# Attention heads paired by parity in 64x32 and 32x32 tiles of TensorE, part of the vector work on GpSimd in slots 24 to 103, and a Prelu step in the weight conversion

## The chip, the cores and the metric

One Trainium2 chip, of which the kernel uses one core. The metric is the time of one execution on the device in microseconds (us). In the text PE is TensorE, DVE is VectorE, ACT is ScalarE, POOL is GpSimd, SP is SyncE.

## The reference, cut to what matters

q, k and v have the shape (4, 8, 576, 64): 4 batches, 8 heads, 576 tokens, 64 columns. The attention result feeds two feed-forward layers whose weights are 64-bit floats in memory (512x2048 and 2048x512 each).

```python
q_lm = q.reshape(B, H, 32, 18, D).mean(axis=3)      # k_lm likewise
A = sm(q, k_lm); Bm = sm(q_lm, k_lm); C = sm(q_lm, k)   # sm: softmax of scaled scores
Z = Bm.transpose(0, 1, 3, 2) / (norm1(Bm) * norminf(Bm) + 1e-06)
for _ in range(6):
    Z = 2 * Z - Z @ Bm @ Z
x = (A @ Z @ C @ v)                 # tokens x 512
h = x @ w_in;  x = (h - tanh(h)) @ w_out            # first layer
h = x @ w_in2; x = (h * tanh(softplus(h))) @ w_out2 # second layer, the output
```

## The kernel before, in words

**Phase 1** is a pipeline of 128 slots, 32 for each batch: two halves of 288 tokens by 16 blocks of 128 hidden columns. The product A (Z C v) w_in is folded: for each batch and block of 512 hidden columns P = (Z C v) w_in is made per head, and h of a slot is P times the softmax A. Slot s makes h(s) with six matmuls of 128x288 (L489 to L491, in the type fp32r, each factor split into a high and a low part) and, with a lag of three slots, y(s-3) with twelve (L589, L590, L593) that accumulate over the 16 blocks. The vector work of a slot (`vec`) makes h - tanh h: ACT squares h (L539), takes its tanh (L540), an exponential (L542) and a square (L553); DVE makes a mask for small h (L545), h times its square (L549), h - tanh h (L550, which is also the last reader of the PSUM bank of h, of which there are two), and for the slot before the product L567 and the choice by the mask, L571. For slot s-2 the result g is split for the y matmuls: ACT writes the high part (L94), DVE the low one (L95, tile `gg`).

**Beside it** run parts of the attention for the next half or batch, as generators of which one piece is issued in a slot. `attn_pre` takes means of q and k (L220), makes the scores of the landmarks (L254), their softmax, C v in 32-wide column tiles (L339), and inverts Bm by Newton's steps: five iterations of L365, a 128x128 matmul of 192 columns for each of the two groups of four heads, and DVE's update L368. The four heads of a group stand in a block-diagonal matrix (L328). `attn_a` makes the scores of A (L404), and the softmax with a subtraction and a multiplication on GpSimd (L419, L431) and a split whose low part is GpSimd's too (L439, which calls L95). `p_gen` makes one P for a batch, a group and a block of 512 columns (L461, then ACT L469 and DVE L471); it runs in slots 1, 2, 5, 6 and 27, 28, 30, 31 of a batch.

**Weights** come as pairs of 32-bit words. A conversion makes fp32 of 128x512 of them: ACT takes the high words (L118) and the low ones (L122), DVE joins them in two scalar_tensor_tensor instructions (STT, L129 and L133). Of the 64 conversions 32 lie in the first 130 us, before and in slots 0 to 14, six in slots 105 to 122, and 26 in phase 2. Weights of w_out, and both weights of the second layer, are then split, the low part on GpSimd (L95).

**Phase 2** is the second layer in 96 slots of 384 tokens by 128 hidden columns, from 486 us on; its inputs are split by L778 with GpSimd.

**Order.** Up to slot 115 a list scheduler places the instructions on each engine, with higher priority for the split of gg, L567, L571 and ACT's exponential and square. From slot 116 (`SWITCH`) they stand as written.

Of the kernel before, what the change touches and what calls it, by code (L numbers as in the profile page):

```python
# [27 lines left out]
def kernel(  # L28
# [16 lines left out]
    M = 32  # L45
# [42 lines left out]
    G = nc.gpsimd  # L88

# [25 lines left out]

    def f32_a(raw, on_act):
        y = st_p.tile([128, 512], F32, tag="y", name="y")
        A.activation(out=y, in_=raw.bitcast(F32)[:, :, 1], func=ACTF.Copy, scale=2.0 ** -112)  # L118
# [7 lines left out]
        return y, lo  # L126

    def f32_b(y, lo, t):
# [4 lines left out]
        V.scalar_tensor_tensor(  # L133
            out=t.bitcast(U32), in0=y.bitcast(U32), scalar=0x80000000, in1=lo,
            op0=ALU.bitwise_and, op1=ALU.bitwise_or,
        )
        yield 0

    def split_job(src, pool, tag, dst, i):
        def done(y):  # L140
            w = pool.tile([128, 2, 512], F32R, tag=tag, name=tag)
            split(y, w[:, 0, :], w[:, 1, :], G)
            dst[i] = w
        return src, done, None

    def keep_job(src, g, j, a):
# [5 lines left out]
        def done(y):  # L152
            if a == 1:
                nc.sync.dma_start(out=w1s[g, j], in_=w1t[0, g, j])
                ready.append((g, j))
        return src, done, where

    def convert(jobs, act_share=1, more=None):
# [10 lines left out]
        for i in range(n + 2):  # L169
            if i < n:  # L170
                st[i], los[i] = f32_a(raws.pop(i), i % act_share == 0)
            if i - 1 in los:
                where = jobs[i - 1][2]
                yield from f32_b(st[i - 1], los.pop(i - 1), where() if where else st[i - 1])
# [7 lines left out]
    QB, KB, Z0 = [], [], []  # L182

    def setup_bd():
        for i in range(2):
            for lst, nm in ((QB, "qb"), (KB, "kb")):
                z = bd_p.tile([128, 4, 32], F32, tag=f"{nm}{i}", name=nm)
                G.memset(z, 0.0)
                lst.append(z)
        z = bd_p.tile([128, NG, 2, 64], F32, name="z")  # L190
        G.memset(z, 0.0)
        Z0.append(z)
# [21 lines left out]
    def attn_pre(b):  # L214
# [8 lines left out]
        def scaled(g, x):  # L223
            if x == 0:
                A.activation(out=ks[g][:, :, S:S + M], in_=red[:, g, 0], func=ACTF.Copy, scale=1.0 / R)
            for i in range(2):
                ps = slice(64 * i, 64 * i + 64)
                adone.add((b, g, "kq"[x]))
                A.activation(out=(KB, QB)[x][g][ps, i:4:2, :], in_=red[ps, g, x], func=ACTF.Copy, scale=1.0 / R)
# [17 lines left out]
        for hf in range(2):  # L247
            pp = []
            for g in range(NG):
                inp[b, g]["c"] = c[:, g]  # L250
                p = ps_m.tile([128, 512], F32, tag="m", name="m")
                qf = QB[g].rearrange("p a c -> p (a c)")
# [3 lines left out]
                pp.append(p)  # L256
# [50 lines left out]
        for g in range(NG):  # L307
# [18 lines left out]
        BD = sm_p.tile([128, 2 * NG, 4, M], F32, tag="BD", name="BD", bufs=1)  # L326
        bbv = bb.rearrange("p t (g o) m -> p (t g) o m", o=1)
        V.tensor_tensor(out=BD, in0=bbv.to_broadcast([128, 2 * NG, 4, M]),  # L328
                        in1=mask.rearrange("p (o a) m -> p o a m", o=1).to_broadcast([128, 2 * NG, 4, M]), op=ALU.mult)
# [3 lines left out]
        for g in range(NG):  # L333
            vv = inp[b, g]["v"]
            for j in range(5):
                n = 128 if j < 4 else 64
                for i in range(4):
                    c4 = slice(32 * i, 32 * i + 32)
                    mm(pv[c4, 64 * g:64 * g + 64], cts[g][0:n, j, c4], vv[0:n, j, 64 * i:64 * i + 64],  # L339
# [8 lines left out]
        yv = sm_p.tile([128, NG, 192], F32, tag="yv", name="yv", bufs=2)  # L348
        for g in range(NG):
            A.activation(out=yv[:, g, 128:192], in_=pv[:, 64 * g:64 * g + 64], func=ACTF.Copy,  # L350
# [3 lines left out]
        for g in range(NG):  # L354
            bt = BD[:, NG + g].rearrange("p a m -> p (a m)")
            mm(py[:, 128 * g:128 * g + 128], bt, bt, start=True, stop=True)
        yield 1
        nr = n4.rearrange("p t (g o) -> p t g o", o=1)[:, 3]
        V.tensor_tensor(out=yv[:, :, 0:128], in0=py[:, 0:256].rearrange("p (g n) -> p g n", g=NG),
                        in1=nr.to_broadcast([128, NG, 128]), op=ALU.mult)  # L360
        yield 1
        for it in range(5):
            pn = ps_m.tile([128, 512], F32, tag="m", name="m")
            for g in range(NG):
                mm(pn[:, 192 * g:192 * g + 192], yv[:, g, 0:128], yv[:, g], start=True, stop=True)  # L365
            yield 1
            y2 = sm_p.tile([128, NG, 192], F32, tag="yv", name="yv", bufs=2)
            V.scalar_tensor_tensor(out=y2, in0=yv, scalar=2.0, in1=pn[:, 0:192 * NG].rearrange("p (g n) -> p g n", g=NG),  # L368
# [4 lines left out]
        for g in range(NG):  # L373
            mm(pn[:, 64 * g:64 * g + 64], yv[:, g, 0:128], yv[:, g, 128:192], start=True, stop=True)
        yield 1
        v6 = sm_p.tile([128, NG, 64], F32, tag="v6", name="v6", bufs=1)
        V.scalar_tensor_tensor(out=v6, in0=yv[:, :, 128:192], scalar=2.0,
# [511 lines left out]
```

## Time and profile before

| | before |
|---|---|
| median of 3 runs | 889.87 us (885.38 to 890.6) |
| profiled execution, its own time | 888.02 us |
| span of the profiled execution | 886.1 us |
| PE busy | 834.0 us (94%) |
| DVE busy | 559.6 us (63%) |
| ACT busy | 512.8 us (58%) |
| POOL busy | 138.3 us (16%) |
| moved by DMA | 79.54 MB |

The busy time of an engine is summed over the whole span, so a share over the span says little about a kernel with stages: DVE's 63% is nearly all in the first 486 us. The table by stretches in the rows below is the view to begin with. In the rows, L12 is line 12 of the kernel before; x is a count of records; a matmul in fp32 leaves two records. PEclk is the granted clock of TensorE, 1.00 being the higher of its two levels, 2.4 GHz.

### The profile page before, as it was taken

How to read it: one execution, taken by the hardware profiler on the slowest of the kernel's cores; microseconds unless marked ns; L12 is line 12 of the kernel's file. 1: busy time of each engine (PE TensorE's matmuls, PEld its weight loads, DVE VectorE, ACT ScalarE, POOL GpSimd, SP SyncE). 2: the span in 40 equal slices, each digit the busy share in tenths (PEclk: the TensorE clock that was granted, in tenths of full speed). 3: DMA queues.
4: the chain of work that ended last, by engine and by line, in shares of the span. 5: the costliest groups of instructions: out<-in, count | busy, mean ns of one | idle time of the engine just before them, and what ended most of it. 6: DMA issues, size and time to landing. Idle time of an engine off the chain costs nothing.

```text
span 886.1 us, 13841 instructions
## 1 busy us (share of the span) xinstructions
PE 834.0 (94%) x5080; PEld 721.3 (81%) x5080; DVE 559.6 (63%) x1268; ACT 512.8 (58%) x1254; POOL 138.3 (16%) x131
## 2 busy tenths in 40 slices
PE   4678779999999999999889999999999999999998
PEld 2444669878997889878789978998998999899896
DVE  7898999999999999999995698611111111111111
ACT  6688977787877887789876667432311311311311
POOL 1431310220002100222310355411100100100000
PEclk8579999999999999999999999999999999999999
DMA  8788603151404300152201555101200200200000
GB/s 294 244 269 313 245 7 129 60 168 45 135 1 132 140 1 28 49 170 63 84 1 47 198 186 188 45 32 31 71 1 1 73 1 1 63 1 0 36 1 36
DMA packets 34916, 79.54 MB, mean 90 GB/s; under 512 B 5408, under 2 KB 14112, under 8 KB 34848
## 3 DMA queue, kind: packets, MB, share of 16 engines
q1 hardware_dynamic: 34848, 78.66, 26.7%
q8 instruction: 40, 0.66, 0.3%
q14 instruction: 28, 0.23, 0.1%
HBM read 65.01 MB, written 13.63 MB: 89 GB/s over the span
## 4 chain that ended last, share of the span: by engine, by line
PE 76%; DVE 14%; ACT 4%; DMA 2%; issue 2%; SPq 0%; POOL 0%; DVEq 0%; ACTq 0%
PE y L589 7%; PE y L617 6%; PE y L613 6%; PE y L612 6%; PE y L593 6%; PE y L590 6%; PE h L513 5%; PE h L515 5%; PE h L514 5%; PE h L489 3%; PE h L490 3%; PE h L491 3%; PE m L461 3%; DVE y L133 2%; PE m L515 2%; PE m L513 2%
## 5 line engine op out<-in xcount | busy, mean ns | idle before, releaser
L560 DVE TENSOR_TENSOR gg<-g,gg 128x384 fp32r<-128x384 f32 x96 | 58.3, 607 | 285.6 <-ACT g L559 285.3
L589 PE MATMUL y<-gg,w 128*128 128x288 f32 x512 | 151.4, 311 | 0.7 <-ACT gg L94 0.6
L590 PE MATMUL y<-gg,w 128*128 128x288 f32 x512 | 143.5, 296 | 0.0
L589 PEld LDWEIGHTS y<-gg,w 128*128 128x128 f32 x512 | 96.4, 188 | 30.4 <-issue 26.1
L593 PE MATMUL y<-gg,w 128*128 128x288 f32 x512 | 109.6, 299 | 5.7 <-DVE gg L95 5.6
L558 ACT ACTIVATE gg<-h 128x384 fp32r<-128x384 f32 x66 | 32.4, 491 | 125.8 <-PE h L515 125.8
L613 PE MATMUL y<-w,gg 128*128 128x512 f32 x256 | 101.2, 395 | 0.0
L612 PE MATMUL y<-w,gg 128*128 128x512 f32 x256 | 100.8, 394 | 0.0
L590 PEld LDWEIGHTS y<-gg,w 128*128 128x128 f32 x512 | 96.9, 189 | 0.8 <-issue 0.8
L593 PEld LDWEIGHTS y<-gg,w 128*128 128x128 f32 x512 | 81.5, 189 | 12.1 <-DVE gg L95 8.3
L617 PE MATMUL y<-w,gg 128*128 128x512 f32 x256 | 88.4, 396 | 0.0
L489 PE MATMUL h<-AT,P 128*128 128x288 f32 x256 | 78.5, 307 | 7.8 <-DVE th L550 7.4
L94 ACT ACTIVATE gg<-g 128x288 fp32r<-128x288 f32 x128 | 56.8, 444 | 39.0 <-PE y L593 25.2
L491 PE MATMUL h<-AT,P 128*128 128x288 f32 x256 | 76.4, 299 | 1.4 <-DVE P L471 1.4
L490 PE MATMUL h<-AT,P 128*128 128x288 f32 x256 | 76.4, 298 | 0.0
L553 ACT ACTIVATE q<-q,bias_c 128x288 f32<-128x288 f32 x128 | 68.6, 536 | 2.3
L539 ACT ACTIVATE s<-h 128x288 f32<-128x288 f32 x128 | 52.3, 409 | 29.0 <-PE h L491 28.6
L95 POOL TENSOR_TENSOR w<-y,w 128x512 fp32r<-128x512 f32 x32 | 49.5, 1547 | 118.3 <-ACT w L94 118.2
L513 PE MATMUL h<-yc,wj 128*128 128x384 f32 x192 | 64.7, 337 | 2.8 <-ACT g L559 2.7
L558 ACT ACTIVATE gg<-m 128x384 fp32r<-128x384 f32 x30 | 14.8, 492 | 89.2 <-PE m L515 89.2
L95 DVE TENSOR_TENSOR gg<-g,gg 128x288 fp32r<-128x288 f32 x128 | 64.0, 500 | 3.4 <-ACT gg L94 2.8
L515 PE MATMUL h<-yc,wj 128*128 128x384 f32 x192 | 64.6, 337 | 0.0
(152 smaller groups left out, 1968.4 us busy)
## 6 DMA issues: line engine op xcount, KB each, us to landing
w<-w1s SPq DMA_DIRECT2D x24, 512.0 KB, 3.3
raw<-in_w1i_dram SPq DMA_DIRECT2D x16, 512.0 KB, 4.9
raw<-in_w1o_dram SPq DMA_DIRECT2D x16, 512.0 KB, 4.3
raw<-in_w2i_dram SPq DMA_DIRECT2D x16, 512.0 KB, 3.8
raw<-in_w2o_dram SPq DMA_DIRECT2D x16, 512.0 KB, 3.8
k<-in_kT_dram SPq DMA_DIRECT2D x8, 576.0 KB, 4.7
q<-in_qT_dram SPq DMA_DIRECT2D x8, 576.0 KB, 4.3
ys<-raw SPq DMA_DIRECT2D x16, 288.0 KB, 3.6
```

What stands on the lines that cost most here:

```text
L95: eng.tensor_tensor(out=L, in0=src, in1=f32(H), op=ALU.subtract)
L489: mm(p, P[:, g, 0, c], AT[:, g, 0, :], start=(g == 0), stop=False)
L490: mm(p, P[:, g, 0, c], AT[:, g, 1, :], start=False, stop=False)
L491: mm(p, P[:, g, 1, c], AT[:, g, 0, :], start=False, stop=(g == NG - 1))
L513: mm(p, w[:, 0, k, :], y[:, k, 0, :], start=(k == 0), stop=False)
L515: mm(p, w[:, 1, k, :], y[:, k, 0, :], start=False, stop=(k == 3))
L589: mm(yps[d], w[:, 0, c], gg[:, 0, :], start=(f == 0), stop=False)
L590: mm(yps[d], w[:, 1, c], gg[:, 0, :], start=False, stop=False)
L593: mm(yps[d], w[:, 0, c], gg[:, 1, :], start=False, stop=(f == NF - 1))
L612: mm(p, gg[:, 0, cs], w[:, 0, :], start=(f == 0), stop=False)
L613: mm(p, gg[:, 0, cs], w[:, 1, :], start=False, stop=False)
L617: mm(p, gg[:, 1, cs], w[:, 0, :], start=False, stop=(f == NF - 1))
```

## The change

Heads are put in two sets by parity. The two heads that share a 128-partition tile go to two PSUM tiles, one for each half of the partitions, and a function `blocks` issues eight tiles of 64x32 (64 contraction rows, 32 columns of weights) at the positions (64e, 32c). It serves the landmark scores (L254 before), the scores of A (L404) and P (L461) for both groups at once; P is made at i = 3, 6 and 28, 31 of a batch's slots, with two loads of w1 issued together. A function `heads` issues four tiles of 32x32 on the diagonal of TensorE for a Newton step, all of which write one PSUM tile, so that yv shrinks from 192 to 96 columns a group and the block-diagonal matrix is needed for one product only. The zeroed tiles that held block-diagonal operands are no longer needed, nor their memsets.

A function `E` returns GpSimd in slots 24 to 103 and DVE otherwise. It decides for the split of gg, the mask, the two softmax steps and the split of A, and the splits of weights (which all lie outside slots 24 to 103, and so go to DVE); the split of phase 2's inputs goes to DVE.

In the first 38 conversions ACT's step is a Prelu with slope 2^32 for negative values in place of a copy, so that the sign lands where the first STT needs it, and the second STT is left out.

The diff, cut to its core:

```diff
+    def E():
+        return G if 24 <= cur[0] < NS - 24 else V
...
+        if one:
+            A.activation(out=y, in_=hi, func=ACTF.Prelu, scale=2.0 ** -112, alpha=2.0 ** 32)
+        else:
+            A.activation(out=y, in_=hi, func=ACTF.Copy, scale=2.0 ** -112)
...
+    def f32_b(y, lo, one, t):
         V.scalar_tensor_tensor(
-            out=lo, in0=y.bitcast(U32), scalar=3, in1=lo, op0=ALU.logical_shift_left, op1=ALU.bitwise_or
+            out=t.bitcast(U32) if one else lo, in0=y.bitcast(U32), scalar=3, in1=lo,
+            op0=ALU.logical_shift_left, op1=ALU.bitwise_or,
         )
         yield 0
+        if not one:
+            V.scalar_tensor_tensor(
...
-            split(y, w[:, 0, :], w[:, 1, :], G)
+            split(y, w[:, 0, :], w[:, 1, :], E())
...
+    def blocks(outs, lhs, rhs):
+        for c in range(4):
+            for e in range(2):
+                ps = slice(64 * e, 64 * e + 64)
+                mm(outs[e][32 * c:32 * c + 32], lhs[ps, c, :], rhs(ps, c % 2, c // 2), start=True, stop=True,
+                   tile_position=(64 * e, 32 * c))
+
+    def heads(o, lhs, rhs):
+        for c in range(4):
+            ps = slice(32 * c, 32 * c + 32)
+            mm(o[ps], lhs[ps], rhs[ps], start=True, stop=True, tile_position=(32 * c, 32 * c))
...
-                for a in range(2):
-                    mm(p[64 * a:64 * a + 64, 0:NH], qf[:, 64 * a:64 * a + 64], ks[g][:, a, NH * hf:NH * hf + NH],
-                       start=True, stop=True)
+            blocks([p[:, 0:NH] for p in pp], QB, lambda ps, g, a: ks[g][ps, a, NH * hf:NH * hf + NH])
...
-                mm(pn[:, 192 * g:192 * g + 192], yv[:, g, 0:128], yv[:, g], start=True, stop=True)
+                heads(pn[:, 96 * g:96 * g + 96], yv[:, g, 0:32], yv[:, g])
...
-        for a in range(2):
-            mm(pa[64 * a:64 * a + 64, 0:HS], kf[:, 64 * a:64 * a + 64], q[:, a, HS * hf:HS * hf + HS],
-               start=True, stop=True)
+            blocks([pas[i][:, 0:HS] for i in range(NG)], KB,
+                   lambda ps, i, a: inp[b, i]["q"][ps, a, HS * hf:HS * hf + HS])
...
-        G.tensor_tensor(out=x, in0=x, in1=xm.to_broadcast([128, NB, M]), op=ALU.subtract)
+        E().tensor_tensor(out=x, in0=x, in1=xm.to_broadcast([128, NB, M]), op=ALU.subtract)
...
-        for a in range(2):
-            mm(p[64 * a:64 * a + 64], z[:, a, :], w[:, a, :], start=True, stop=True)
+        blocks(pp, Z0, lambda ps, g, a: ws[g][ps, a, :])
...
-                split(g2, gg[:, 0, :], gg[:, 1, :], V)
+                split(g2, gg[:, 0, :], gg[:, 1, :], E())
...
+            tables["prelu"] = False
...
+                if E() is G:
+                    mask_op(G)
                 new = [
-                    lambda: mask_op(V),
+                    lambda: E() is G or mask_op(V),
...
-                split(t, yc[c][:, k, 0], yc[c][:, k, 1], G)
+                split(t, yc[c][:, k, 0], yc[c][:, k, 1], V)
...
-                if b and i in (1, 2, 5, 6):
-                    streams.append(p_gen(b, (i + 1) % 2, 2 + (i > 2)))
+                if b and i in (3, 6):
+                    streams.append(p_gen(b, 2 + (i > 3)))
...
-                if i in (27, 28, 30, 31):
-                    streams.append(p_gen(b + 1, (i + (i < 29)) % 2, int(i > 29)))
+                if i in (28, 31):
+                    streams.append(p_gen(b + 1, int(i > 28)))
```

What this does to the order of instructions is seen on three engines. On PE, in a slot of the middle stage, before the change one P (m, from the weights w and z) of one group stands behind the L593 of the first half of a y. The numbers in the names w are those of buffers.

```order
L593 MATMUL y<-gg,w 128x288 x2
L461 MATMUL m<-w_2053,z 64x512 x2
L589 MATMUL y<-gg,w 128x288
L590 MATMUL y<-gg,w 128x288
L589 MATMUL y<-gg,w 128x288
```

After the change the eight tiles of both groups stand in one such place (lines of the changed kernel: L211 is in `blocks`, L603, L604 and L607 are the old L589, L590 and L593).

```order
L607 MATMUL y<-gg,w 128x288 x2
L211 MATMUL m<-w_2132,z 32x512 x2
L211 MATMUL m<-w_2134,z 32x512 x2
L211 MATMUL m<-w_2132,z 32x512 x2
L211 MATMUL m<-w_2134,z 32x512 x2
L603 MATMUL y<-gg,w 128x288
L604 MATMUL y<-gg,w 128x288
```

The other group's P, which stood in a slot before, is gone from there: two places became one. On DVE, a stretch of the middle stage before the change holds six instructions of `vec` a slot, among them the split L95 and the mask L545.

```order
L95 TENSOR_TENSOR gg<-g,gg 128x288
L571 COPY_PREDICATED g<-mk,th 128x288
L545 TENSOR_SCALAR mk<-s 128x288
L549 TENSOR_TENSOR g<-h,s 128x288
L550 TENSOR_TENSOR th<-h,th 128x288
L567 TENSOR_TENSOR g<-q,g 128x288
```

After the change DVE has four there (L563, L564, L581 and L585 are the old L549, L550, L567 and L571).

```order
L563 TENSOR_TENSOR g<-h,s 128x288
L564 TENSOR_TENSOR th<-h,th 128x288
L581 TENSOR_TENSOR g<-q,g 128x288
L585 COPY_PREDICATED g<-mk,th 128x288
L563 TENSOR_TENSOR g<-h,s 128x288
L564 TENSOR_TENSOR th<-h,th 128x288
L378 TENSOR_TENSOR yv<-m,n_2916 128x2x32
L581 TENSOR_TENSOR g<-q,g 128x288
```

The other two are in GpSimd's queue, the split of slot s-2 (L100) always ahead of the mask of slot s (L557).

```order
L100 TENSOR_TENSOR gg<-g,gg 128x288
L557 TENSOR_SCALAR mk<-s 128x288
L100 TENSOR_TENSOR gg<-g,gg 128x288
L557 TENSOR_SCALAR mk<-s 128x288
L100 TENSOR_TENSOR gg<-g,gg 128x288
```

Both moved from one queue to the other, in the same slot as before.

## Rows read from the trace of the kernel before

**Rows 1.** Busy time by stretch: stretch, us, busy (records) PE, PEld, DVE, ACT, POOL; PEclk, DMA, GB/s.

```profile
0.00:46.00 46.00, 25.77 (x158) 14.93 (x158) 36.20 (x73) 28.75 (x65) 14.14 (x23) 0.67 0.77 264
46.00:130.00 84.00, 65.71 (x331) 43.48 (x332) 79.59 (x171) 69.59 (x167) 22.00 (x17) 0.92 0.62 216
130.00:410.00 280.00, 280.00 (x2152) 243.12 (x2152) 268.28 (x712) 223.35 (x594) 31.79 (x40) 1.00 0.26 86
410.00:450.00 40.00, 33.35 (x232) 30.85 (x231) 40.00 (x89) 32.27 (x86) 11.35 (x9) 1.00 0.21 68
...
486.00:600.00 114.00, 111.17 (x555) 99.34 (x554) 72.86 (x92) 61.96 (x124) 43.51 (x28) 1.00 0.41 133
```

**Rows 2.** Waits of PE, 410 to 450 us: total us, times, longest.

```profile
PE h L489 <- DVE th L550: 5.7, 7, 1.7
```

**Rows 3.** Timeline of PE around one P: start us, us (of the row), operation, tile.

```profile
264.77 0.43 PE L593 MATMUL y<-gg,w 128*128 128x288 f32 x2
265.13 1.08 PE L461 MATMUL m<-w,z 128*64 128x512 f32 x4
...
266.38 0.30 PE L590 MATMUL y<-gg,w 128*128 128x288 f32 x1
```

**Rows 4.** Timeline of PE around one Newton iteration, which lies between these rows.

```profile
246.47 0.43 PE L593 MATMUL y<-gg,w 128*128 128x288 f32 x2
...
247.53 0.29 PE L590 MATMUL y<-gg,w 128*128 128x288 f32 x1
```

**Rows 5.** Groups of PE by form, 130 to 410 us: busy us, mean ns | idle before.

```profile
L461 PE MATMUL m<-w,z 128*64 128x512 f32 x96 | 25.7, 614 | 0.0
L365 PE MATMUL m<-yv 128*128 128x192 f32 x60 | 12.3, 327 | 0.0
L404 PE MATMUL m<-q,kb 128*64 128x288 f32 x48 | 8.5, 432 | 0.0
L254 PE MATMUL m<-k,qb 128*64 128x304 f32 x32 | 6.2, 442 | 0.0
```

**Rows 6.** Timeline of DVE in one slot of the middle stage.

```profile
374.79 0.44 DVE L95 TENSOR_TENSOR gg<-g,gg 128x288 fp32r<-128x288 f32 x1
375.15 0.30 DVE L545 TENSOR_SCALAR mk<-s 128x288 uint8<-128x288 f32 x1
375.37 0.45 DVE L549 TENSOR_TENSOR g<-h,s 128x288 f32<-128x288 f32 x1
...
376.10 0.45 DVE L567 TENSOR_TENSOR g<-q,g 128x288 f32<-128x288 f32 x1
```

**Rows 7.** Groups of POOL by form, whole span.

```profile
L95 POOL TENSOR_TENSOR AT<-c,AT 128x288 fp32r<-128x288 f32 x14 | 11.7, 838 | 28.2 <-ACT AT L94 28.2
```

**Rows 8.** Timelines of POOL and DVE where both are at work.

```profile
360.74 0.73 POOL L419 TENSOR_TENSOR c<-c,xm 128x288 f32<-128x288 f32 x1 [61.32 <-ACT gg L94]
...
360.86 0.92 DVE L95 TENSOR_TENSOR gg<-g,gg 128x288 fp32r<-128x288 f32 x1
...
375.34 0.81 POOL L95 TENSOR_TENSOR AT<-c,AT 128x288 fp32r<-128x288 f32 x1 [1.71 <-ACT AT L94]
```

**Rows 9.** Timeline of DVE, 412 to 450 us: first and last of eight over 0.9.

```profile
412.56 1.04 DVE L129 SCALAR_TENSOR_TENSOR raw<-y,raw 128x512 uint32<-128x512 uint32 x1
...
444.99 1.40 DVE L545 TENSOR_SCALAR mk<-s 128x288 uint8<-128x288 f32 x1
```

**Rows 10.** Groups of DVE by form, 0 to 130 us.

```profile
L129 DVE SCALAR_TENSOR_TENSOR raw<-y,raw 128x512 uint32<-128x512 uint32 x32 | 24.6, 771 | 4.4 <-ACT raw L122 4.1
...
L133 DVE SCALAR_TENSOR_TENSOR y<-y,raw 128x512 uint32<-128x512 uint32 x16 | 13.6, 853 | 0.2
L133 DVE SCALAR_TENSOR_TENSOR w<-y,raw 128x512 uint32<-128x512 uint32 x16 | 11.1, 697 | 0.0
```

**Rows 11.** The conversion's step on ACT by form, 0 to 130 us.

```profile
L118 ACT ACTIVATE y<-raw 128x512 f32<-128x512 f32 x32 | 21.4, 669 | 5.8 <-DMA raw<-in_w1i_dram 3.5 <-DMA raw<-in_w1o_dram 2.0
```

**Rows 12.** The squares of slots 24 to 103: count, ns least, median, most; starts.

```profile
L539 ACT ACTIVATE s<-h x80: 388/412/434, 167.4 to 416.0; 128x288 f32<-128x288 f32 x80
```

More of the change, by code (lines that the diff above doesn't have):

```diff
@@ L114, in raw_f32 @@
         return f32(raw_p.tile([128, 512, 2], U32, tag="raw", name="raw").rearrange("p f t -> p (f t)"))
+    tables = {"prelu": True}
     def f32_a(raw, on_act):
         y = st_p.tile([128, 512], F32, tag="y", name="y")
-        A.activation(out=y, in_=raw.bitcast(F32)[:, :, 1], func=ACTF.Copy, scale=2.0 ** -112)
+        hi = raw.bitcast(F32)[:, :, 1]
+        one = tables["prelu"]
+        if one:
+            A.activation(out=y, in_=hi, func=ACTF.Prelu, scale=2.0 ** -112, alpha=2.0 ** 32)
+        else:
+            A.activation(out=y, in_=hi, func=ACTF.Copy, scale=2.0 ** -112)
         lo = raw[:, :, 0]
@@ L181 @@
     w1t = {}
[L182 to L192, printed above, removed]
+    QB = bd_p.tile([128, 4, M], F32, name="qb")
+    KB = bd_p.tile([128, 4, M], F32, name="kb")
+    Z0 = bd_p.tile([128, 4, M], F32, name="z")
+    def blocks(outs, lhs, rhs):
[8 more added lines that the diff above has]
+            mm(o[ps], lhs[ps], rhs[ps], start=True, stop=True, tile_position=(32 * c, 32 * c))
     ATt = {}
@@ L225, in scaled @@
                 A.activation(out=ks[g][:, :, S:S + M], in_=red[:, g, 0], func=ACTF.Copy, scale=1.0 / R)
[L226 to L229, printed above, removed]
+            adone.add((b, g, "kq"[x]))
+            A.activation(out=(KB, QB)[x][:, g:4:2, :], in_=red[:, g, x], func=ACTF.Copy, scale=1.0 / R)
         todo = []
@@ L325, in attn_pre @@
         yield 0
[L326 to L329, printed above, removed]
+        BD = sm_p.tile([128, NG, 4, M], F32, tag="BD", name="BD", bufs=1)
+        bbv = bb[:, 0].rearrange("p g (o m) -> p g o m", o=1)
+        V.tensor_tensor(out=BD, in0=bbv.to_broadcast([128, NG, 4, M]),
+                        in1=mask.rearrange("p (o a) m -> p o a m", o=1).to_broadcast([128, NG, 4, M]), op=ALU.mult)
         yield 1
@@ L347, in attn_pre @@
         yield 0
-        yv = sm_p.tile([128, NG, 192], F32, tag="yv", name="yv", bufs=2)
+        yv = sm_p.tile([128, NG, 96], F32, tag="yv", name="yv", bufs=2)
         for g in range(NG):
-            A.activation(out=yv[:, g, 128:192], in_=pv[:, 64 * g:64 * g + 64], func=ACTF.Copy,
+            A.activation(out=yv[:, g, 32:96], in_=pv[:, 64 * g:64 * g + 64], func=ACTF.Copy,
                          scale=n4[:, 2, g:g + 1])
@@ L430, in attn_a @@
         yield 0
[L431 removed]
+        E().tensor_tensor(out=x, in0=x, in1=xm.to_broadcast([128, NB, M]), op=ALU.mult)
         yield 1
@@ L451, in w1_load, with p_gen @@
             nc.sync.dma_start(out=t, in_=w1s[g, j])
-    def p_gen(b, g, j):
-        w = w1t.pop((b, g, j))
-        if g == 0:
-            Pt[b, j] = P_p.tile([128, NG, 2, 512], F32R, tag="P", name="P")
-        P = Pt[b, j]
-        p = ps_m.tile([128, 512], F32, tag="m", name="m")
-        z = ZT[b, g]
-        for a in range(2):
-            mm(p[64 * a:64 * a + 64], z[:, a, :], w[:, a, :], start=True, stop=True)
-        n = 2 * (4 * b + j) + g + 2
-        if b:
+    def p_gen(b, j):
+        ws = [w1t.pop((b, g, j)) for g in range(NG)]
+        P = Pt[b, j] = P_p.tile([128, NG, 2, 512], F32R, tag="P", name="P")
+        pp = [ps_m.tile([128, 512], F32, tag="m", name="m") for g in range(NG)]
+        blocks(pp, Z0, lambda ps, g, a: ws[g][ps, a, :])
+        n = 2 * (4 * b + j) + 2
+        if b or j == 3:
             w1_load(n)
-        elif j == 3 and g == 1:
-            w1_load(n - 1)
-            w1_load(n)
+            w1_load(n + 1)
         yield 1
-        A.activation(out=P[:, g, 0, :], in_=p, func=ACTF.Copy)
-        yield 0
-        V.tensor_tensor(out=P[:, g, 1, :], in0=p, in1=f32(P[:, g, 0, :]), op=ALU.subtract)
-        done.add((b, g, j))
+        for g, p in enumerate(pp):
+            A.activation(out=P[:, g, 0, :], in_=p, func=ACTF.Copy)
+            yield 0
+            V.tensor_tensor(out=P[:, g, 1, :], in0=p, in1=f32(P[:, g, 0, :]), op=ALU.subtract)
+            yield 0
+            done.add((b, g, j))
         yield 1
```

82 lines of the change are left out of this document (37 added, 45 removed).

## The prediction

> **What bounds the kernel now.** I read first the busy time of every engine by stretch [rows 1], then what PE waits for in the stretches where it is not full, then the timeline around single groups of matmuls. The reader should see four stages with different limits. From 0 to 130 us no engine is full: DVE is busy 115.8 of 130 (36.20 + 79.59), ACT 98.3, PE 91.5, and the DMA engines 62 to 77%. From 130 to 410 PE is busy 280.00 of 280: the stage lasts as long as PE has work. DVE is close behind, 268.28, with 11.7 us of slack; GpSimd does 31.8 us. From 410 to 450 DVE is busy 40.00 of 40 and PE has 6.65 us of holes, of which 5.7 is a wait for DVE's subtraction at L550, which frees the PSUM bank of h [rows 2]. From 486 to 600 PE lacks 2.8 us, and after that nearly nothing. So what the change takes from PE counts in the middle stage, and what it takes from or adds to DVE counts at the beginning and in 410 to 450; in the middle stage DVE may become the bound.
>
> **PE in the middle stage, what the new tiles remove.** The matmuls of one group follow each other in fixed steps: two L593 take 0.43 and one 0.30, so a step of 288 columns is 0.13 us [rows 3]. After the two L593 that begin at 264.77 and one L589, L590 was due at 264.77 + 3 x 0.13 = 265.16, and began at 266.38: one P (four records at L461, two 64-wide column tiles of 512 columns, two passes each) costs PE 1.22 us. Read in the same way, one Newton iteration (L365, both groups) costs 247.53 - 246.86 = 0.67 [rows 4]. It moves 2 x 192 columns without changing the tile size, 1.74 ns a column; with that, 512 columns of P leave 0.33 us for the change of tile size and back. That gives 0.83 for the 288 columns of one L404 and 0.86 for the 304 of L254; their records (432, 442 against 614 ns for P) are in that order [rows 5]. In the stage there are 24 P (96 records of 4), 12 L404, 8 L254 and 15 iterations [rows 5].
>
> After the change eight tiles of 64x32 serve both groups in one go. If all eight run side by side, a pair costs what a single one did: P 12 x 1.22 = -14.6, L404 6 x 0.83 = -5.0, L254 4 x 0.86 = -3.4. Eight tiles are also eight weight loads and two to four times as many instructions; 0.05 for each of the 22 pairs, an estimate, gives back 1.1. Newton's iteration becomes 2 x 96 columns, but now with a change of tile size: 0.33 + 0.33 = 0.66 against 0.67, nothing. Side by side is not shown for row tiles by any row; L339 runs four column tiles only. The bounds are therefore -22 (all parallel) and +7.7 (nothing parallel across rows, worked out with the rivals). I take -22, since the column tiles of P already do run side by side: two of 512 columns in 0.89. PE would need 258 us for the work of this stage.
>
> **DVE in the middle stage, what GpSimd takes over and what that costs.** In slots 24 to 103 the split of gg (L95) and the mask (L545) leave DVE: 374.79 to 375.15 and 375.15 to 375.37, 0.36 + 0.22 = 0.58 a slot [rows 6]. 80 x 0.58 = 46.4, and halved Newton operands give some 2 more: DVE goes from 268 to 220. GpSimd gets 80 splits of 128x288 at 0.838 [rows 7] and 80 masks, of which it has no row: the lower bound is DVE's own 0.30 [rows 6], the upper 0.838 of an operation with two inputs. I take 0.5, as one input is nearer to the first: 80 x 1.34 = 107 us, beside the 32 it has, in 258. That fits on GpSimd.
>
> It does not fit freely beside DVE. At 360.86 DVE's L95 took 0.92, against 0.44 at 374.79, while GpSimd's subtraction ran from 360.74 to 361.47; but a GpSimd split from 375.34 to 376.15 left the two that read PSUM as they are: L549 took 0.45 from 375.37, L550 followed, and the next began 0.73 after it [rows 6, 8]. So operations on SBUF alone exclude each other, and those with a PSUM operand do not. Left on DVE in a slot are two that read PSUM (together 0.73, from 375.37 to 376.10) and two that don't (L567, L571). How much of GpSimd's time DVE loses is bounded by nothing and all of it, 0 and 107. From 410 to 450, where DVE always has something queued, eight instructions from the first [rows 9] to the last took over 0.9 us, 6.7 us more than their kinds take, against 11.35 us of GpSimd: a share of 0.59. In the middle stage DVE has gaps, and 0.73 us of each slot's 1.34 can lie under the PSUM operations, which leaves 0.61, or 0.45. I take 0.4: 43 us, DVE 220 + 43 = 263, against PE's 258. The stage then lasts 263: **-17** (bounds -22, where PE decides, and the rivals).
>
> The Trainium skill ("GPSIMD Engine Reference", section 4.1, Engine selection) has GpSimd at half of VectorE's pace for two inputs, and about equal for one. By that the mask would take 0.30, DVE 220 + 0.4 x 91 = 256, PE's 258 would decide, and the sum would end 5 us lower.
>
> Queued behind the moved work: GpSimd takes the split of slot s-2, then the mask of slot s, so the mask waits where the split waits for ACT, and DVE's copy_predicated (L571) of the next slot for the mask. The matmuls wait for the split three slots after its h, as before, so one late split costs nothing while h (two PSUM banks) is still drained by DVE.
>
> **0 to 130 us.** The second STT of 32 conversions goes (L133, 0.85, and 0.70 where it writes w) [rows 10]. An instruction's successor starts 0.08 before its end (0.44 against 0.36), so 32 x 0.69 = -22. ACT's Prelu has no row; its bounds are nothing and twice Copy's 0.67 [rows 11], and I take Copy's, as the same elements pass. 16 splits of w come from GpSimd to DVE, 0.36 x 512/288 = 0.64, +10.2, and 12 operations of attention, +4.3; L129 (0.77 for 512 columns, 0.64 + 0.08 by the same scale) stops waiting for GpSimd, 0.04 x 32 = -1.3. Net -9 of DVE. DVE is full only in pieces here, with ACT and DMA behind it, but a shorter conversion also ends sooner, and P waits for it. **-9**, bounds 0 (ACT or DMA take over) and -18 (the 84.00 - 65.71 that PE idles from 46 to 130).
>
> **410 to 450 us.** The six conversions lose an STT each, -6 x 0.69, six splits and three of yc join DVE, about +5, and the 6.7 us lost beside GpSimd go: -6 of DVE. PE's holes are 6.65. **-5**, bounds 0 and -6.6. **486 to 600:** the splits go to DVE, which has 41 us free; **-1**, bounds +2 and -2.8. From 600 on nothing.
>
> **Sum,** against the profiled 888.0 (the median of the runs is 889.9, 0.2% more): -9 - 17 - 5 - 1 = -32, **856 us**.
>
> **Rivals.** *Newton's row tiles take turns.* The four diagonal tiles of an iteration write one PSUM bank. Then 4 x 192 columns at 1.74 + 0.33 = 1.67, +1.0 x 15 = +15; PE's stage is 273, above DVE's 263, so -7: 866. For it: no row shows row tiles. Against it: nothing either, but that the columns of P overlap. The Trainium skill ("TensorEngine Tiling (Array Packing)", Gotcha 1: PSUM Pressure) says that different row tiles cannot access the same bank at once; no run here shows it yet, and by it this would be the outcome.
> *No row tiles run side by side,* so the change doesn't do what it says. P 12 x (1024 x 1.74 + 0.33 = 2.11) = 25.3 for 29.3, L404 8.0 for 10.0, L254 5.6 for 6.9: -7.3, and Newton's +15: PE 287.7, +7.7, total 881.
> *DVE becomes the bound.* At the share of 0.59, 220 + 63 = 283, +3 in place of -17: 876. For it: DVE would have as little slack as from 410 to 450. Against it: two of four operations in a slot read PSUM.
> *Slower.* One mechanism: GpSimd's queue alternates so that nearly all its time falls on DVE's SBUF operations. At all of 107 us DVE needs 327, +47: 920. It decides from a share of about 0.8 on (306, 899 us). Against it: 0.59 where DVE was full.
>
> **How the numbers follow.** Forecast 0.63, its own range 838 to 866 (PE bound in the middle and more gain at the start, or a share of 0.5); Newton in turns 0.10; no row tiles 0.06; DVE the bound 0.14; slower 0.07. Within 1% (about what a measurement of this kernel can tell from no change) is 881 to 899. Faster: 0.63 + 0.10 + half of no row tiles 0.03 + 0.10 of DVE's = 0.86. Within: 0.03 + 0.04 + 0.02 = 0.09. Slower: 0.05. The range 838 to 880 leaves out slower (0.07), 0.03 and 0.04 of the two before it, and 0.04 of a better start: 0.18.
>
> **What the profile after would show.** The 80 squares at L539 that now take 248.6 us from first to last [rows 12] should take about 233. One pair of P should put the next matmul off by 1.22 to 1.3; 2.1 would mean turns, and an iteration of 1.67 would mean the first rival. GpSimd's split should be near 0.84 and its mask 0.3 to 0.5; means of L567 and L571 well above 0.45 would show DVE losing time to GpSimd, and PE waits for the PSUM drain in slots 24 to 103 that DVE is the bound. From 410 to 450 no instruction of DVE should take over 0.9. The forecast is wrong if PE shows large waits in the middle, or if PE is full there but no shorter.

## The result and the profile after

The changed kernel took 864.42 us (median of 4 runs, 861.34 to 865.87) against 889.93 before (4 runs, 885.38 to 890.6): a ratio of 0.972, 95% interval 0.968 to 0.976. The forecast was 856, its range 838 to 880. The profiled execution took 864.62, its span is 862.8, which is 23.3 less than before. DVE's busy time fell from 559.6 to 501.6 us, GpSimd's rose from 138.3 to 174.3.

The squares at the start of the slots (L539 before, L551 after) cut the span into stages that can be compared. From slot 128 on, where there is no square, the first of ACT's activations of 384 columns in a slot (L558, L572) stands for it. In us:

| from square to square | before | after | difference | forecast for about this stage |
|---|---|---|---|---|
| span's start to slot 24 | 154.4 | 152.0 | -2.4 | -9 |
| slot 24 to 104 | 252.4 | 240.3 | -12.1 | -17 |
| slot 104 to 128 | 67.7 | 62.5 | -5.2 | -5 |
| slot 128 to the end | 411.7 | 408.0 | -3.7 | -1 |

The squares of slots 24 to 103, which answer [rows 12], in the view of one line (least, median and most ns; first and last start):

```profile
L551 ACT ACTIVATE s<-h x80: 385/412/478, 152.0 to 390.1; 128x288 f32<-128x288 f32 x80
```

They span 238.1 us; it was 248.6, and 233 was named as the sign. The busy time by stretch of the changed kernel, columns as in [rows 1]:

```profile
0.00:46.00 46.00, 26.55 (x281) 13.42 (x285) 30.20 (x76) 28.00 (x63) 0.68 (x6) 1.00 0.80 266
46.00:130.00 84.00, 68.32 (x450) 44.67 (x443) 70.10 (x173) 66.32 (x164) 0.00 (x0) 0.94 0.64 216
...
390.00:427.00 37.00, 34.52 (x250) 33.10 (x249) 36.64 (x96) 33.95 (x91) 1.76 (x2) 1.00 0.22 67
...
462.00:576.00 114.00, 114.00 (x579) 103.18 (x578) 69.70 (x121) 64.83 (x130) 0.00 (x0) 1.00 0.44 137
```

From 0 to 130 DVE has 100.3 us of work where it had 115.8 [rows 1], GpSimd next to none, and yet slot 24 begins only 2.4 us earlier. In slots 104 to 128 (third row) PE's holes shrank to 2.5 of 37. At the beginning of phase 2 (last row) PE is full where it lacked 2.8. The same view for slots 24 to 104 alone, first of the kernel before, then of the changed one:

```profile
154.40:406.70 252.30, 252.30 (x1881) 215.84 (x1880) 241.05 (x638) 201.95 (x537) 30.14 (x39) 1.00 0.25 83
```

```profile
152.00:392.00 240.00, 237.46 (x2219) 207.80 (x2218) 204.77 (x480) 193.22 (x527) 173.26 (x196) 1.00 0.27 91
```

DVE is busy 204.8 of 240 and PE 237.5: DVE has 35 us to spare, and PE is nearly full. The timeline of PE around a pair of P, the answer to [rows 3], and around a Newton iteration, the answer to [rows 4]:

```profile
229.48 0.43 PE L607 MATMUL y<-gg,w 128*128 128x288 f32 x2
229.84 0.53 PE L218 MATMUL m<-yv 32*32 32x96 f32 x16
230.30 0.40 PE L603 MATMUL y<-gg,w 128*128 128x288 f32 x1
230.54 0.29 PE L604 MATMUL y<-gg,w 128*128 128x288 f32 x1
...
258.59 0.42 PE L607 MATMUL y<-gg,w 128*128 128x288 f32 x2
258.94 1.09 PE L211 MATMUL m<-w,z 64*32 64x512 f32 x16
259.96 0.40 PE L603 MATMUL y<-gg,w 128*128 128x288 f32 x1
260.20 0.30 PE L604 MATMUL y<-gg,w 128*128 128x288 f32 x1
```

L604 was due at 258.59 + 3 x 0.13 = 258.98 and began at 260.20: a pair of P, eight tiles, costs 1.22 us, exactly what a single P cost. In the same way an iteration in sixteen records of 32x32 tiles costs 230.54 - 229.87 = 0.67 (0.66 with the finer step below). GpSimd's two new operations by form (busy, mean ns):

```profile
L557 POOL TENSOR_SCALAR mk<-s 128x288 uint8<-128x288 f32 x80 | 77.3, 966 | 7.2 <-ACT s L551 0.7 <-POOL gg L100 0.2
L100 POOL TENSOR_TENSOR gg<-g,gg 128x288 fp32r<-128x288 f32 x80 | 69.0, 862 | 206.1 <-ACT gg L99 204.3
```

Where PE stands still between plain 288-column matmuls was read from the starts of its successive instructions. In slots 24 to 104 these holes are 1.2 us before and 8.9 after; 1.4 of the 8.9 is one hole at the very end, where PE waits for L564 to drain h. The work on other tiles, with the changes of tile size and the waits inside it, was 61.2 before and 41.8 after. With 80 x 18 steps of 0.1316 (189.5) this closes: 251.9 and 240.2.

### The profile page after: what moved, and what is told of

It is laid out like the page before. It is cut to its first block, busy times and chain, and to the rows that moved or that the text cites. A ratio compares the mean times of both kernels' runs of the same rounds, so it can differ in the third digit from the quotient of the medians.

```text
span 862.8 us, 14979 instructions
## 1 busy us (share of the span) xinstructions
PE 817.7 (95%) x5656; PEld 708.2 (82%) x5656; DVE 501.6 (58%) x1154; ACT 497.1 (58%) x1234; POOL 174.3 (20%) x202
## 4 chain that ended last, share of the span: by engine, by line
PE 77%; ACT 9%; DVE 7%; POOL 3%; issue 2%; DMA 1%; SPq 0%; DVEq 0%; ACTq 0%; POOLq 0%
PE y L631 7%; PE y L627 7%; PE y L626 7%; PE y L603 6%; PE h L526 5%; PE h L525 5%; PE h L524 5%; PE y L607 5%; PE y L604 5%; PE m L211 4%; PE h L500 3%; PE h L501 3%; PE h L502 3%; PE m L526 2%; PE m L525 2%; PE m L524 2%
## 5 line engine op out<-in xcount | busy, mean ns | idle before, releaser
L574 DVE TENSOR_TENSOR gg<-g,gg 128x384 fp32r<-128x384 f32 x96 | 53.5, 558 | 275.6 <-ACT g L573 275.6
L603 PE MATMUL y<-gg,w 128*128 128x288 f32 x512 | 151.6, 311 | 5.8 <-ACT gg L99 4.2
L604 PE MATMUL y<-gg,w 128*128 128x288 f32 x512 | 143.7, 296 | 0.0
L603 PEld LDWEIGHTS y<-gg,w 128*128 128x128 f32 x512 | 97.0, 189 | 30.7 <-issue 14.8
L607 PE MATMUL y<-gg,w 128*128 128x288 f32 x512 | 110.1, 300 | 1.9 <-DVE gg L100 1.5
L100 POOL TENSOR_TENSOR gg<-g,gg 128x288 fp32r<-128x288 f32 x80 | 69.0, 862 | 206.1 <-ACT gg L99 204.3
L572 ACT ACTIVATE gg<-h 128x384 fp32r<-128x384 f32 x66 | 32.5, 492 | 132.6 <-PE h L526 132.5
L604 PEld LDWEIGHTS y<-gg,w 128*128 128x128 f32 x512 | 97.3, 190 | 0.8 <-issue 0.8
L607 PEld LDWEIGHTS y<-gg,w 128*128 128x128 f32 x512 | 81.7, 190 | 8.1 <-DVE gg L100 3.8
L557 POOL TENSOR_SCALAR mk<-s 128x288 uint8<-128x288 f32 x80 | 77.3, 966 | 7.2 <-ACT s L551 0.7
L585 DVE COPY_PREDICATED g<-mk,th 128x288 f32<-128x288 uint8 x128 | 72.8, 569 | 4.6
L567 ACT ACTIVATE q<-q,bias_c 128x288 f32<-128x288 f32 x128 | 69.1, 540 | 2.2
L563 DVE TENSOR_TENSOR g<-h,s 128x288 f32<-128x288 f32 x128 | 57.3, 448 | 21.5 <-ACT th L552 20.9
L551 ACT ACTIVATE s<-h 128x288 f32<-128x288 f32 x128 | 52.4, 410 | 27.2 <-PE h L502 25.8
L572 ACT ACTIVATE gg<-m 128x384 fp32r<-128x384 f32 x30 | 14.8, 492 | 89.3 <-PE m L526 89.3
```

What stands on the lines that cost most here:

```text
L557: eng.tensor_scalar(out=mk, in0=e, scalar1=FT, scalar2=None, op0=ALU.is_ge)
L567: A.activation(out=q, in_=q, func=ACTF.Square, scale=FB, bias=bias_c[:, 0:1])
L585: V.copy_predicated(out=g0, mask=mk0, data=t0)
L603: mm(yps[d], w[:, 0, c], gg[:, 0, :], start=(f == 0), stop=False)
L604: mm(yps[d], w[:, 1, c], gg[:, 0, :], start=False, stop=False)
L607: mm(yps[d], w[:, 0, c], gg[:, 1, :], start=False, stop=(f == NF - 1))
```

## Experiments

Each run's stages, in us, in the order of the runs below (medians of all its executions in the last column; "slot 24" counts from the span's start):

| kernel | slot 24 at | 24 to 104 | 104 to 128 | 128 to 160 | median |
|---|---|---|---|---|---|
| before | 154.4 | 252.4 | 67.7 | 135.9 | 888 to 890 |
| changed | 152.0 | 240.3 | 62.5 | 132.3 | 864.4 |
| tiles alone | 160.0 | 245.6 | 67.4 | 135.8 | 884.4 |
| all but the tiles | 147.5 | 250.2 | 63.7 | 132.3 | 871.0 |
| Prelu alone | 148.5 | 251.8 | 64.6 | 135.9 | 878.6 |
| all on DVE | 153.1 | 254.1 | 66.4 | 132.2 | 883.2 |
| all on DVE, order as written | 151.0 | 266.2 | 81.3 | 132.2 | 910.2 |
| masks on DVE | 155.8 | 242.7 | 63.3 | 132.3 | 868.6 |
| half of a conversion step on DVE | 151.6 | 240.3 | 62.4 | 132.3 | 865.6 |
| conversions in another order | 156.1 | 240.4 | 62.4 | 132.3 | 866.7 |
| second half's attention a slot later | 148.5 | 240.4 | 62.3 | 132.3 | 861.9 |
| the same, next batch's too | 149.3 | 243.8 | 61.8 | 132.3 | 864.4 |
| the same, P at 29 | 147.0 | 241.8 | 63.4 | 132.3 | 861.8 |
| the same, attention all on DVE | 146.3 | 240.5 | 62.7 | 132.3 | 861.2 |

**How far the first column holds.** One execution of each kernel was profiled. Four of these kernels (the changed one, all on DVE, the same as written, masks on DVE) have the same order of instructions on PE, DVE, ACT and GpSimd up to slot 20, and yet that slot begins at 139.9, 141.1, 138.9 and 143.7 us. So a difference of less than 5 us at the start, seen in one execution a side, shows little by itself. The later columns are firmer: from slot 24 to the end the changed kernel and the three that differ from it by half of a conversion step, by the order of conversions or by the second half's attention take 710.7 to 710.9. With the medians of the runs in place of the profiled times, and everything from slot 24 on as profiled, the start differs from before by -4.7 with the whole change (-2.4 in the table), -7.6 with all but the tiles (-6.9), -7.8 with Prelu alone (-5.9) and +3.1 with the tiles alone (+5.6).

**The parts alone.** First the tiles without the rest.

```diff
-    tables = {"prelu": True}
+    tables = {"prelu": False}
...
-        return G if 24 <= cur[0] < NS - 24 else V
+        return V
...
-            split(y, w[:, 0, :], w[:, 1, :], E())
+            split(y, w[:, 0, :], w[:, 1, :], G)
```

(and G again for the two softmax steps, the split of A and that of phase 2's inputs)

> Only the new tiles (scores, P, Newton) on the kernel before; DVE and GpSimd keep the work they had, and the second STT stays. What decides is the time from the square of slot 24 to that of slot 104: 252.4 us before, 240.3 with the whole change. Theory: PE loses about 20 us of work there, but DVE, which had 268 of 280 before, is then the bound, so 244 to 250 us and 878 in total. Rival: PE alone decides, 233 us and 868.

884.4 us, ratio 0.995 (0.993 to 0.997): nearly nothing, though the stretch of slots 24 to 104 fell to 245.6, as the theory had it. DVE is busy 236.4 us of that stretch, and the largest waits of PE there are for DVE, 5.6 us for the split of gg and 2.7 for P: it is late at some places and nearly full. The start lost 5.6 us (3.1 by the medians), which neither side had foreseen. Then everything but the tiles: the kernel before with `E` and the Prelu step.

> The kernel before with the change's GpSimd rule and its Prelu conversion, but with the old tiles. Theory: PE stays full from slot 24 to 104, so that stretch keeps its 252 us, whatever DVE and GpSimd do; what remains are the gains outside of it, 2 at the start, 5 in slots 104 to 128 and 4 in phase 2: 879. Rival: the late splits of GpSimd cost PE as much here as they seem to with the new tiles (8 us of holes in that stretch): 887.

871.0, ratio 0.980 (0.978 to 0.982). The stretch kept 250.2 of 252.4, as the theory said: with old tiles PE is full there, whatever DVE does. But slot 24 began 6.9 us earlier than before, against 2.4 with the whole change. So the conversions and splits do bring at the start about what was forecast, and the paired tiles take 4.5 us of it back (2.9 by the medians; 3.5 to 8.3 for the four executions of the same start above). The Prelu step alone:

```diff
+            A.activation(out=y, in_=hi, func=ACTF.Prelu, scale=2.0 ** -112, alpha=2.0 ** 32)
...
-        V.scalar_tensor_tensor(out=t.bitcast(U32), in0=y.bitcast(U32), scalar=0x80000000, in1=lo,
-            op0=ALU.bitwise_and, op1=ALU.bitwise_or)
```

> The kernel before with the Prelu conversion alone; tiles and GpSimd's work as before. Up to slot 24 the run with Prelu and the GpSimd rule on old tiles gained 6.9 us, in slots 104 to 128 it gained 4.0. Theory: most of the start's gain is the second STT (32 x 0.69 of DVE), most of the other stretch's is that DVE no longer stands behind GpSimd's splits: here 5 us at the start, 1 to 2 in slots 104 to 128, nothing elsewhere, 882. Rival: the start's gain too comes from the splits that GpSimd no longer makes beside DVE: 1 to 2 us at the start, 886.

878.6, ratio 0.988 (0.985 to 0.991), somewhat more than the theory had: 5.9 us at the start and 3.1 in slots 104 to 128. ACT's Prelu takes what Copy took: 672 ns in the changed kernel against 669 [rows 11]. Only the runs in which phase 2's splits are off GpSimd have 132.2 or 132.3 for slots 128 to 160; the two with GpSimd there (tiles alone, Prelu alone) have 135.8 and 135.9.

**Is GpSimd's part needed?** The changed kernel with `E` returning DVE always:

> The changed kernel with its rule returning DVE in all slots: GpSimd does nothing but the identity. Theory: DVE gets back 80 times 0.58 us and 36 attention operations of 0.36, less what it lost to GpSimd, and is the bound from slot 24 to 104: 248 to 255 us there, 873 to 880 in total. Rival: the exclusion costs DVE about as much as GpSimd takes over, so the stretch stays at 238 to 242 and the total at 862 to 866.

883.2, and 254.1 us in slots 24 to 104, more than before the change, with all its tiles. The stretch is what the theory named, the total is above it. But DVE was not full:

```profile
153.10:407.20 254.10, 250.88 (x2212) 209.31 (x2210) 234.93 (x670) 194.19 (x525) 0.00 (x0) 1.00 0.24 81
```

PE shows 250.9 busy. What filled it is seen in its timeline, one P of this run:

```profile
172.77 0.30 PE L604 MATMUL y<-gg,w 128*128 128x288 f32 x1
173.00 1.04 PE L211 MATMUL m<-w,z 64*32 64x512 f32 x2
173.97 0.53 PE L607 MATMUL y<-gg,w 128*128 128x288 f32 x2
174.43 1.08 PE L211 MATMUL m<-w,z 64*32 64x512 f32 x14
175.44 0.40 PE L603 MATMUL y<-gg,w 128*128 128x288 f32 x1
```

The sixteen records stand in two places, two and fourteen, with y's matmuls between, and each part lasts as long as a whole pair: a tile of 512 columns takes its time whether it runs alone or beside seven others. Of the 22 pairs of the stretch 12 are torn like this, in two or three places. Over the stretch the work on other tiles was about 61 us, against 41.8 in the changed kernel. In `blocks` the second tile is the first that needs the second PSUM bank; that the list scheduler cut there because that bank came free later is likely, but not shown. So the forecast's picture, PE's work fixed and DVE beside it, was incomplete: the order decides whether the pairs save anything. Whether whole pairs would be enough was asked with the order as written from slot 24 on:

```diff
-    SWITCH = 116
+    SWITCH = 24
```

> The run with everything on DVE, but with the order as written from slot 24 on, not from 116. In that run DVE was busy 235 of 254 us, PE had only 3 us of holes, yet 19.6 us more went to other tiles than in the changed kernel: the list scheduler had torn 11 of 21 pairs into two places, and each part of a P cost 1.17. Theory: in written order the pairs are whole again, that work falls back to about 42 us, and DVE's 235 us with some waits decide: 240 to 246 us from slot 24 to 104, 870 to 876 in total. Rival: DVE cannot keep up, and the time goes to waits in place of torn pairs: 252 to 256 us, 882 or more.

910.2, ratio 1.025 (1.021 to 1.030), 266.2 us in the stretch: the rival, and 10 us worse than it had it. The pairs were whole, and the time went to waits, spread over many:

```profile
151.00:417.00 266.00, 243.40 (x2217) 208.34 (x2216) 241.18 (x676) 192.80 (x519) 0.00 (x0) 0.99 0.25 86
```

```profile
PE y L607 <- DVE gg L100: 6.8, 6, 1.5
PE m L211 <- DMA w<-w1s: 5.5, 2, 3.1
PE m L218 <- DVE yv L387: 2.8, 2, 1.4
```

DVE's split of gg comes first, then the loads of w1, which the written order leaves too late for P. DVE is busy 241 of 266, so "DVE cannot keep up" is right in the sense of being late, not of being full. Whole pairs alone don't make up for GpSimd's part; how much of it is the order is not separated by this run. The other way round, only the masks back on DVE:

> The changed kernel with the masks of slots 24 to 103 back on DVE, where one costs 0.22 from start to start; on GpSimd it took 0.97, more than the 0.5 of the prediction. Theory: DVE has about 37 us free in that stretch, takes 18 of them, and GpSimd blocks it 77 us less, so the holes of PE there (8 us) shrink to 4 or less: 236 us, 860 in total. Rival: DVE is crowded where the attention's pieces lie, and the masks add to it: 243 us and 867.

868.6, 242.7 us in the stretch: the rival. Moving 77 us of GpSimd's time away and giving DVE 18 made it slower, so GpSimd's hold on DVE was not what cost most. The holes did shrink, from 8.9 to 6.4, but the pairs that wait for DVE grew by more: three pairs of scores took 2.48 in place of 1.63, two of landmark scores 1.90 in place of 0.87.

**What holds the start?** Two guesses, both from the chain of waits. Half of the low words' shifts to DVE (`convert(jobs, 2)`):

> The changed kernel, in which every second conversion of the first 32 has its low words shifted by DVE and not by ACT. Up to the square of slot 24 the change gained 2.4 us where the prediction had 9. Theory: ACT's conversion steps took the place of DVE's (11.3% and 11.1% of the chain of waits between 88 and 118 us), so moving 16 x 0.55 us of them back to DVE ends slot 24 some 3 to 5 us earlier: 860. Rival: the start is held by P, which waits for both groups, and DVE is still nearly full: 0 to 2 us later, 865.

865.6, slot 24 at 151.6 and not at 152.0: nothing. ACT stands often in the chain there, but taking these shifts from it doesn't help. And the conversions of the second block of w_in earlier:

> The changed kernel with the conversions of the second block of w_in ahead of seven of w_out that are needed later, so that both groups' weights for the second P are there long before slot 4. Theory: up to slot 24 the paired P cost 4.5 us (slot 24 begins at 152.0 us, at 147.5 with the old tiles), because a pair starts only when the later group's weights are converted; the step at slot 4 (10.5 us, 5.8 with the old tiles) shrinks by 3 to 5 us, 861. Rival: what holds P is the two PSUM banks that it needs at once, or ACT; slot 24 stays at 151 to 152 us, 864.

866.7, slot 24 at 156.1: the theory fell. The step of slot 4 did shrink, from 10.5 to 6.1 us, but slot 0 began 3.8 us later, and the step of slot 8 grew from 8.3 to 10.9: no gain came of it. That it is slower is less sure, 2.3 us by the medians.

**Where the holes of slots 24 to 104 are.** One is a pair of scores behind a P (the first weight load and matmul, and what they waited for):

```profile
176.02 1.28 DVE L481 TENSOR_TENSOR P<-m,P 128x512 fp32r<-128x512 f32 x2
...
176.76 0.14 PEld L211 LDWEIGHTS m<-q,kb 64*32 64x32 f32 x2 [0.36 <-DVE P L481]
176.76 1.31 PE L211 MATMUL m<-q,kb 64*32 64x288 f32 x16
177.35 0.18 PEld L211 LDWEIGHTS m<-q,kb 64*32 64x32 f32 x14 [0.46 <-DVE P L481]
```

A pair needs both spare PSUM banks, and DVE is still emptying them of P. Three such cost 1.63 in place of 0.85. Another is of another kind, in the slot of the P of i = 28: GpSimd's split of A holds DVE's L585, which ends 0.6 late, two P subtractions follow, and the y matmuls wait for gg:

```profile
167.95 0.81 POOL L100 TENSOR_TENSOR AT<-c,AT 128x288 fp32r<-128x288 f32 x1 [0.30 <-ACT AT L99]
167.99 1.11 DVE L585 COPY_PREDICATED g<-mk,th 128x288 f32<-128x288 uint8 x1
...
169.22 0.40 PE L603 MATMUL y<-gg,w 128*128 128x288 f32 x1 [0.37 <-ACT gg L99]
```

So the pieces were moved apart:

```diff
-                if i == 0:
+                if i == 1:
                     gens["al"] = both(attn_a, b, 1)
-                if i < 7:
+                if 1 <= i < 8:
```

> The changed kernel with the second half's attention (its first piece is a pair of scores) begun one slot later, i = 1 in place of 0, so that it no longer follows at once on the P of i = 31. Theory: the three pairs of scores that took 1.63 us in place of 0.85 waited for the two PSUM banks that DVE was still emptying of P; they go back to 0.85 and the stretch of slots 24 to 104 to 238 us: 862. Rival: the pieces collide with the P of i = 3 in place of it, and nothing is gained: 864 to 866.

861.9, ratio 0.970 (0.967 to 0.973). The six pairs of scores now take 0.85 each, and yet the stretch lasts 240.4: two pairs of landmark scores take 2.08 for 0.87, and other waits grew. The gain came where it had not been looked for: slot 24 begins at 148.5, 3.5 us earlier (2.4 by the medians). It is more than chance: this kernel, P at 29 and attention all on DVE have one order up to slot 20, and begin that slot at 136.4, 134.9 and 134.3, all ahead of the four executions of the order before it (138.9 to 143.7). Two more arrangements, and one with less on GpSimd, each on top of this one:

```diff
-                if i >= 5:
+                if i >= 6:
                     streams.append(gens["a"])
```

> The changed kernel with both attention streams one slot later: the second half's from i = 1, the next batch's from i = 6 in place of 5. With the first alone the landmark scores of i = 11 waited (2.08 us for 0.87) and the P of i = 28 was still followed by 0.75 us of holes, since the split of A on GpSimd lies in the same slot. Theory: what waits is only the order of the pieces that share the two PSUM banks and DVE; moved together they are 1.2 and 0.75 us a batch better: 235 to 237 us from slot 24 to 104, 857 to 859. Rival: each piece meets another one a slot later, 240 us, 862.

864.4, 243.8 us: the rival, a little worse. P at i = 29 and 31 in place of 28 and 31:

> The changed kernel with the second half's attention from i = 1 and the first P of the next batch at i = 29 in place of 28, a slot behind GpSimd's split of A. Theory: the 0.75 us of holes after the P of i = 28 go, three times, and the landmark scores' wait stays: 238 us from slot 24 to 104, 860. Rival: the P of 29 and of 31 are now so close that the second waits for the first's banks: 241 us, 863.

861.8, 241.8: the rival again. And E() replaced by DVE in the softmax steps and the split of A:

> The run with the second half's attention from i = 1, and with the two softmax steps and the split of A on DVE in every slot; GpSimd keeps the split of gg and the masks. From slot 24 to 104 DVE was busy 205 of 240 us, so it has room for 36 x 0.36 = 13 us, and GpSimd does 28 us less. Theory: most of PE's 7 us of holes there hang on a DVE instruction held by GpSimd's attention work (L585 took 1.11 where its median is 0.50, in the slot of the P of i = 28); they shrink to 4: 237 us, 859. Rival: the holes come from DVE's pieces of attention and of P lying in a row, and more of them on DVE makes it worse: 243 us, 865.

861.2, ratio 0.970 (0.967 to 0.972), 240.5 us: the holes changed their cause and kept their size. The waits of PE in that stretch, of this run:

```profile
PE h L500 <- DVE th L564: 5.2, 5, 1.1
PE y L603 <- ACT gg L99: 0.5, 1, 0.5
```

GpSimd's lateness is gone, and in its place DVE drains the banks of h late, around i = 5 of each batch and i = 7 of two, where its own pieces of attention and P lie. Of the five arrangements, the changed kernel's own among them, three end at 240.3 to 240.5 and none lower; why they meet there is not settled. The best medians (861.2 to 861.9) lie at the lower edge of the changed kernel's runs (861.3 to 865.9), so the totals alone don't show them faster than the change; the profiles show the start 2.6 to 5.6 us shorter, the medians 2.4 to 5.0.

## Why the forecast was near, and where it was off

**PE's work: right.** -22 us were forecast for P, scores and Newton in the middle stage. Measured between slots 24 and 104: -19.4 of work on other tiles, in which the waits of three score pairs count 2.4 the other way, so -21.8 without them. A pair of P is 1.22 (forecast 1.22 to 1.27), an L404 pair 0.85 (0.83), an L254 pair 0.87 (0.86), an iteration 0.66 (0.66). The 0.05 a pair for weight loads and instructions stood on no row; the pairs show 0.02 or less.

**The rival of Newton in turns fell.** The measurement decides against the Trainium skill ("TensorEngine Tiling (Array Packing)", Gotcha 1: PSUM Pressure), by which different row tiles can't access one bank at once: the four diagonal tiles write one bank, and an iteration takes 0.66, not 1.67. By the columns too: products of 32, 64 and 96 columns for both groups cost 0.45, 0.55 and 0.66, 3.3 ns a column. Two groups one after the other, each with its four tiles side by side, would give 2 x 1.74 = 3.5, and tiles in turns four times that. The rival that no row tiles run side by side fell with P's 1.22.

**DVE in the middle stage: the wrong quantity.** The step "263, against PE's 258; the stage then lasts 263" added up DVE's busy time. DVE was busy 204.8 of 240 between slots 24 and 104, and the two operations beside GpSimd lost little: L581 took 0.50 and L585 0.62 on average, against averages of 0.45 and 0.48 in the run with all on DVE, where GpSimd is idle, so 79 x (0.05 + 0.14) = 15 us, a share of 0.09 of GpSimd's 173 and not 0.4. L563 and L564, which read PSUM, kept 0.45, as the prediction had it. The mask on GpSimd cost 0.97, not 0.5, and 0.838 was no upper bound; that didn't matter either. What PE lost, about 10 us (7.7 more holes and the 2.4 in the score pairs), is local: all but the 1.4 at the end of the stretch stands at the three turns of a batch, i = 28 to 6, where P, pieces of attention and two PSUM banks meet. A loss of 5 us was forecast for a reason that didn't hold, so it is luck that the -17 lies as near to -12 as it does.

**0 to 130 us: the term that was mis-sized.** -9 was taken for "net -9 of DVE". That part is right: with the old tiles these edits bring 6.9. What was not in the sum is that paired P and scores cost 4.5 there (2.9 by the medians). In that stage the pairs are torn: between slots 0 and 24 the changed kernel's P stand in ten places of 2 to 10 records, none of them less than 1.18 us, against nine places before and ten with all but the tiles. So they saved nothing: the work on other tiles with its waits was 38.1 us against 38.7 before and about 35 with all but the tiles. But tearing isn't what they cost. Moving one stream by a slot, with P in the same ten places, brought slot 20 from 138.9 to 143.7 down to 134.3 to 136.4, about where all but the tiles has it (135.4). So the loss hangs on the order of the other pieces around P; which of the waits in it is first is not settled, nor what PE's lower pace adds (last section).

**410 to 450 us: right.** -5 was forecast, -5.2 came, mostly by the reason given: Prelu alone brings 3.1, the rest of the edits on old tiles 0.9 more (63.7), and the last 1.2, which the sum didn't have, comes with the tiles. The sign named came too: no instruction of DVE takes over 0.9 us there, where eight did; with Prelu alone, where GpSimd still splits, seven do. **Phase 2: -1 forecast, -3.7 measured.** Nearly all of it comes from the splits on DVE, 135.9 to 132.2 or 132.3 for slots 128 to 160 in every run that has them there.

**The sum** came out at -23.3 of the span for -32: 6.6 of the difference are the start and 4.9 the middle, less 2.7 in phase 2 and 0.2 in slots 104 to 128. By the medians the start missed by about 4.

## What to carry to other kernels

Small matmul tiles side by side cost as much as one of them, so packing pays in full, but only if all of them are issued in one go: look in the order of the instructions whether a scheduler tears the group, and count the PSUM banks that it needs at once. An engine's total says little about a stage in which it has 35 us to spare: PE waits where bursts meet, so price a moved instruction by what lies next to it there. A part that is worth nothing alone (tiles 0.5%) can carry part of the whole, so measure the parts both alone and left out. Look also how far an equal order of instructions repeats before a difference is explained: here the start differs by 5 us between four executions of one order.

## What the runs showed of the hardware

The mask, one input and a byte output, took 0.93 at the least on GpSimd, longer than a subtraction of two inputs of the same size (0.80 at the least), and 0.30 on DVE [rows 6].

From 20 to 40 us, where Newton's steps of the first batch lie, the column of the granted clock has 0.50 (1.2 GHz) with the old tiles and 1.00 (2.4 GHz) with the new ones. Before, and after:

```profile
20.00:40.00 20.00, 13.63 (x109) 9.30 (x108) 16.57 (x35) 13.39 (x27) 9.47 (x8) 0.50 0.76 254
```

```profile
20.00:40.00 20.00, 14.96 (x206) 9.52 (x206) 14.07 (x43) 14.38 (x32) 0.00 (x0) 1.00 0.66 214
```

The matmuls themselves don't show this difference. In the changed kernel eight transposes of that stretch took 1.94 us and a Newton iteration's records 0.86; in its middle stage the same took 1.03 and 0.53 (the latter in the timeline around a Newton iteration above). In the kernel before, the eight transposes just ahead of that stretch took 1.97.

```profile
18.41 1.97 PE L288 MATMUL m<-ident,c 128*128 128x128 f32 x8 [3.50 <-ACT c L277]
```

```profile
20.92 1.94 PE L307 MATMUL m<-ident,c 128*128 128x128 f32 x8 [4.37 <-ACT c L296]
...
32.94 0.86 PE L218 MATMUL m<-yv 32*32 32x96 f32 x16 [0.85 <-DVE yv L387]
...
216.80 1.03 PE L307 MATMUL m<-ident,c 128*128 128x128 f32 x8
```

So PE ran there well below its later pace in the changed kernel too, and the column alone doesn't tell the pace: the steps between equal matmuls do. With the tiles alone the column has 1.00 as well, and slot 0 began at 51.4 us, against 51.6 before. Up to slot 24, h and y matmuls that follow each other 0.24 us apart, not 0.13, number 17 before, 24 after, 21 with all but the tiles, 56 with the tiles alone, 58 with the masks on DVE and 67 with the conversions in another order. At 0.11 each that is 4.3 us more with the tiles alone than before, where the start was 5.6 longer. Whether the lower pace lengthens the start or follows from its waits is not separated by these runs.
